# Gated recurrence and two-layer product: the first batch loaded two chunks at a time

## The chip, the cores and the metric

The kernel runs on one core of a Trainium2 chip. The metric is the device time of one launch in microseconds. A core has five engines with instruction queues of their own: TensorE (PE, with weight loads listed as PEld), VectorE (DVE), ScalarE (ACT), GpSimd (POOL) and SyncE (SP). SP here only issues DMAs, which run on sixteen DMA engines. An instruction waits in its queue for semaphores, and everything behind it on that engine waits with it.

## The reference

Batch 4, heads 8, 768 tokens, head width 48. A recurrence with a forget gate runs over the tokens, and its output goes through two matrices with `h * cos(h)` between them:

```python
f = 1.0 / (1.0 + np.exp(-f_logit))
for t in range(S):
    state = f[:, :, t, :, None] * state + np.einsum('bhd,bhe->bhde', k[:, :, t], v[:, :, t])
    y[:, :, t] = np.einsum('bhd,bhde->bhe', q[:, :, t], state)
x = y.transpose(0, 2, 1, 3).reshape(3072, 384)
h = x @ w_in            # 384 x 2048
out = (h * np.cos(h)) @ w_out   # 2048 x 384
```

## The kernel before

The recurrence is computed in 24 chunks of 128 tokens, six to a batch, numbered from 0 over all batches. For each chunk:

- `decay` loads f_logit and computes on ACT exp, then ln(1 + .), whose running sum over the tokens PE makes (`cum`); ACT then makes the decay factors `b` and their inverses `bi`. This is done for a group of chunks together, since exp and ln need another ACT table than the sine that makes the cosine. Changing the table is an instruction of its own (ACT_TABLE_LOAD).
- `attend` multiplies q by `b` and k by `bi` (`qk`, on POOL or DVE), casts v (`vb` or `vp`), turns q and k (`tr` on PE and a copy `qkt`, or a DMA transpose `tq`), multiplies them (`sc`), masks (`am`, on DVE), makes the state's update (`ps`, `st`, `sz`) and the output `y`, copies it (`yb`) and turns it to `xT` (`trx` on PE and a copy, or a DMA transpose `ty`).

`moe` takes the turned outputs by units: the first two of 128 tokens, eleven more of 256. For each of several pieces PE makes h (L651), ACT its cosine (L658), DVE the product gT (L661); then PE multiplies by w_out (`o`, L671), and ACT or DVE copies to `ot`, which is stored. The weights arrive as four quarters of each matrix in float32, in the buffers of gT, and are cast to bfloat16 (`wc`) by POOL, DVE or ACT.

Chunks below `NPAIR` = 4 have another layout: two neighbouring tokens stand in one partition, so that a contiguous piece of memory is 384 bytes instead of 192. In this layout each load is split into two DMAs of 64 partitions, four heads each, and v is spread over a zeroed tile `vp` of twice the width.

The order of work is not written by hand. `Plan` holds every operation with a cost for each engine that may do it, a priority from the table `PR`, and its buffers; `run` places them one by one in simulated time, each time choosing the engine whose operation could start first and, within `WINDOW`, the one of lowest priority. The result is a fixed order for each engine, and the program's semaphores then do the rest at run time. `GROUPS` says which chunks share their exponentials: one list entry is a group that ACT does without a cosine between, and its numbers are chunks done in one instruction. `PR["gate"]` names the cosine after which a group may begin, and from group `FREE_GROUPS` on a group waits for all its loads of f. Buffers come from `Slots` and PSUM banks from `Banks`.

```python
GROUPS = [(1, 1, 1), (1,), (2,), (2, 2), (2, 2), (2, 2), (2, 2), (2,)]
UNITS = [128, 128] + [256] * 11
TURN_QK = range(14, 23)
TURN_Y = range(12, 23)
```

`TURN_QK` and `TURN_Y` list the chunks whose q and k, or whose outputs, are turned by DMA.

Of the kernel before, what the change touches and what calls it, by code (L numbers as in the profile page):

```python
# [46 lines left out]
class Banks:  # L47
# [33 lines left out]
    def ap(self, s):  # L81
        t = self.base["tiles"][s // 2]
        return t if self.size == 2 else t[:, (s % 2) * 512:(s % 2) * 512 + 512]
# [33 lines left out]
class Plan:  # L117
# [5 lines left out]
    WINDOW = 60.0  # L123
# [4 lines left out]
    def op(self, name, eng, fn, reads=(), writes=(), prio=0.0, table=None, lat=0.0, grp=None,  # L128
           dma=None):
        o = Op()  # L130
        o.name, o.eng, o.fn, o.prio, o.table = name, eng, fn, prio, table
# [23 lines left out]
    def run(self):  # L155
        free = dict.fromkeys(("PE", "ACT", "DVE", "POOL", "SP"), 0.0)
# [10 lines left out]
        while len(order) < n:  # L167
            cand = []
            for o in ready:
# [18 lines left out]
                for e, cost in o.eng.items():  # L188
                    if e == "ACT" and lock is not None and o.grp != lock and o.table is not None:
                        continue  # L190
                    s = max(at, free[e])
                    sw = self.TABLE if e == "ACT" and o.table not in (None, table) else 0.0
                    if pick is None or s + cost + sw < pick[0]:
                        pick = (s + cost + sw, s, e, cost)
# [8 lines left out]
            if e == "ACT" and o.table is not None:  # L203
                if o.table != table:
                    s += self.TABLE
                table = o.table
                if o.grp is not None:
                    left[o.grp] -= 1
                    lock = o.grp if left[o.grp] else None
# [38 lines left out]
GROUPS = [(1, 1, 1), (1,), (2,), (2, 2), (2, 2), (2, 2), (2, 2), (2,)]  # L248
UNITS = [128, 128] + [256] * 11
NPAIR = 4  # L250
FREE_GROUPS = 1
TURN_QK = range(14, 23)
TURN_Y = range(12, 23)
PR = {
    "at": [-12.29, -6.15, -7.86, -3.54, -3.92, 15.62, -19.28, -37.09, -8.89, 2.67, 9.58, 17.38, 9.92, 20.25,
          -11.32, -1.58, 13.93, 10.35, 34.42, 26.02, 40.51, 24.64, 16.95, 12.68],
    "dec": [-8.47, -57.31, -61.04, -69.2, -28.24, -49.14, -79.64, -48.44],
    "f": [-43.16, -25.03, -22.97, -8.07, -2.31, -6.19, 24.79, 54.63, 17.72, 57.23, 51.15, 47.24, 55.46,
          53.45, 44.74, 80.64, 54.13, 111.71, 112.22, 68.31, 95.05, 72.38, 86.37, 55.7],
    "h": [3.03, 31.23, 1.72, -0.8, 2.61, 9.56, -7.84, 18.41, -24.77, 18.52, 17.84, 12.56, -12.9],  # L260
    "k": [-21.87, -16.94, -7.69, -4.47, -9.06, 6.14, 15.33, 36.65, 25.42, 15.32, 15.8, 44.24, 49.16, 72.37,
          75.37, 80.56, 68.29, 83.23, 95.28, 87.29, 95.57, 100.98, 97.99, 79.82],
    "o": [58.13, 26.04, 22.05, 54.64, 24.66, 21.51, 44.13, 47.06, 68.58, 102.72, 70.22, 82.65, 82.73],
    "tq": [1.37, -18.62, 8.94, -41.89, -22.72, -30.79, -29.34, 13.32, 0.45, 25.45, 44.49, 73.32, 0.51, 38.11,
          -19.6, -35.07, -26.72, -52.99, -63.88, -22.16, -23.59, 5.62, -39.1, -8.27],
    "ty": [-29.44, -2.23, -1.14, -18.62, -50.77, -26.99, -41.9, -38.55, -40.26, -17.32, 25.61, -2.03, 2.74,
          8.38, 49.55, 45.48, 2.91, -0.4, -39.16, -44.82, -2.61, -2.74, -26.93, -15.21],
    "v": [-26.8, -34.27, -11.26, 0.13, 3.34, 10.3, 16.09, 22.38, 43.81, 38.01, 48.41, 44.56, 41.68, 43.68,
          90.07, 49.48, 98.02, 44.19, 100.52, 65.78, 64.72, 77.22, 79.02, 126.2],
    "w_in": [-45.54, -7.28, 5.66, -12.05],  # L270
    "w_out": [6.72, 10.57, 101.81, 165.61],
    "wc": [0.78, -2, -17.61, -40.6, -45.98, 2.72, 16.43, 45.54],
    "gate": [None, None, 1, 1, 5, 20, 28, 36],
}


def build(nc, cpool, ppool, q, k, v, f_logit, moe_w_in, moe_w_out, out):
# [21 lines left out]
    if NPAIR:  # L299
        incl, strict = tl([128, 128], BF16, "incl"), tl([128, 128], BF16, "strict")  # L300
        pmask, half = tl([128, 2, 2, 64], BF16, "pmask"), tl([128, 2], BF16, "half")
    if NPAIR and nc is not None:
# [19 lines left out]
    def zpad(t):  # L322
# [3 lines left out]
    kS = slots("k", 4, [128, H, D], F32)  # L326
    qS = slots("q", 4, [128, H, D], F32)
    vS = slots("v", 4, [128, H, D], F32)
# [3 lines left out]
    qkS = slots("qk", 3, [128, 2, H, 64], zero=zpad)  # L332
    vbS = slots("vb", 4, [128, HD])
    vpS = slots("vp", 3, [128, 2, HD], zero=lambda t: nc.gpsimd.memset(t, 0.0)) if NPAIR else None
# [9 lines left out]
    w_in_bf = tl([128, KM, d_ff], BF16, "w_in_bf")  # L344
    w_out_bf = tl([128, KF, d_model], BF16, "w_out_bf")

    base = {"held": [False] * 8, "free": [0.0] * 8,
            "last": [[] for _ in range(8)], "now": [[] for _ in range(8)],
            "tiles": [ppool.tile([128, 1024], F32, name=f"ps_{i}") for i in range(4)]}
    phS = Banks(base, 2, [0, 2, 4], "ph")  # L350
    scS = Banks(base, 2, [4, 6, 2], "sc")
    p1S = Banks(base, 1, [7, 6, 5, 4, 3, 2], "p1")
# [15 lines left out]
    w_in_v = [Val(ap=w_in_bf[:, :, i * 512:(i + 1) * 512] if nc is not None else None) for i in range(NW)]  # L368
# [23 lines left out]
    def load(t, src, b, c, n, prio, nm):  # L392
        def fn(e):
            tok = src[b, :, c * C:(c + 1) * C, :]
            if n >= NPAIR:
                nc.sync.dma_start(out=t.ap, in_=tok.rearrange("h p d -> p h d"))
                return
            for r in range(2):
                (nc.scalar if e == "ACT" else nc.sync).dma_start(
                    out=t.ap[64 * r:64 * r + 64].rearrange("p (h e) d -> p h (e d)", e=2),  # L400
                    in_=tok[4 * r:4 * r + 4].rearrange("h (p e) d -> p h (e d)", e=2))
        P.op(nm + str(n), {"ACT" if nm == "q" and n == 0 else "SP": 420.0 if n >= NPAIR else 840.0}, fn,
             writes=[t], prio=prio, dma=1000.0 if n >= NPAIR else 720.0)

# [7 lines left out]

    def decay(chunks, g, prio):

        m = len(chunks)
        ft, sp, bt, bi = Val(fS), Val(spS), Val(bS), Val(biS)
        pc = Val(scS if m == 2 else p1S)
        for i, (b, c, n, ld) in enumerate(chunks):
            load(ft.part(lambda a, i=i: a[:, i]), f_logit, b, c, n, PR["f"][n], "f")
        fl = lambda a: a[:, 0:m].rearrange("p m h d -> p (m h d)")  # L420

        first = P.op("exp", {"ACT": act(384 * m, "S")}, lambda e: nc.scalar.activation(  # L422
            out=fl(ft.ap), in_=fl(ft.ap), func=AF.Exp, scale=-1.0),
# [4 lines left out]
        if g >= FREE_GROUPS:  # L428
            for o in firsts[g]:
                o.deps.update(loads)  # L430
        def ln(e):
            o, i_ = sp.ap[:, 0:m, :, 0:D], ft.ap[:, 0:m]
            if chunks[0][2] < NPAIR:
                o = sp.ap.rearrange("p m h d -> p (m h) d").rearrange(
                    "p (e h) d -> p h e d", e=2)[:, 0:4 * m, :, 0:D]
                i_ = i_.rearrange("p m h d -> p (m h) d").rearrange("p (h e) d -> p h e d", e=2)
            nc.scalar.activation(out=o, in_=i_, func=AF.Ln, bias=1.0)  # L437
        P.op("ln", {"ACT": act(384 * m, "S")}, ln, reads=[ft], writes=[sp], prio=prio, table="E", grp=g)
        cut = (lambda i: pc.ap[:, 512 * i:512 * i + 512]) if m == 2 else (lambda i: pc.ap)

        for i in range(m):
            def pe(e, i=i, pair=chunks[i][2] < NPAIR):
                o = cut(i)
                if pair:
                    rows = sp.ap.rearrange("p m h d -> p (m h) d")
                    w = rows.rearrange("p (e h) d -> p h e d", e=2)[:, 4 * i:4 * i + 4]
                    v = o[:, 0:HD].rearrange("p (h e d) -> p h e d", e=2, d=D)
                    nc.tensor.matmul(v, lhsT=incl, start=True, stop=False,  # L448
                                     rhs=w[:, :, 0:1, 0:D].broadcast_to([128, NP, 2, D]))
                    nc.tensor.matmul(v[:, :, 0, :], lhsT=strict, rhs=w[:, :, 1, 0:D], start=False, stop=False)  # L450
                    nc.tensor.matmul(v[:, :, 1, :], lhsT=incl, rhs=w[:, :, 1, 0:D], start=False, stop=False)
                    for p in range(2):
                        for e in range(2):
                            nc.tensor.matmul(o[:, HD + p:HD + NP:2], lhsT=rows[:, 8 * e + 4 * i + 2 * p:8 * e + 4 * i + 2 * p + 2, :].rearrange(
                                                 "p h d -> p (h d)"),
                                             rhs=half, start=False, stop=(p == 1 and e == 1))
# [3 lines left out]
                for p in range(NP):  # L460
                    nc.tensor.matmul(o[:, HD + p:HD + p + 1],
                                     lhsT=sp.ap[:, i, 2 * p:2 * p + 2, :].rearrange("p h d -> p (h d)"),
                                     rhs=umask[:, C - 1:C], start=False, stop=(p == NP - 1))
            P.op("cum", {"PE": 285.0 if chunks[i][2] >= NPAIR else 450.0}, pe, reads=[sp], writes=[pc], prio=prio)
# [10 lines left out]
    def attend(b, c, n, ld, bt, bi, i, prio):  # L475
        kf, qf, vf = ld
        pm = n < NPAIR
        qk, vb = Val(qkS), Val(vpS if pm else vbS)
        E = lambda e: nc.vector if e == "DVE" else nc.gpsimd
        for j, (src, dec) in enumerate(((qf, bt), (kf, bi))):  # L480
            P.op("qk", {"POOL": 1150.0, "DVE": 640.0} if n < 4 else {"POOL": 1150.0},
                 lambda e, j=j, src=src, dec=dec: E(e).tensor_mul(  # L482
                out=qk.ap[:, j, :, 0:D].rearrange("p (e h) d -> p h e d", e=2) if pm else qk.ap[:, j, :, 0:D],
                in0=src.ap.rearrange("p (h e) d -> p h e d", e=2) if pm else src.ap,
# [285 lines left out]
```

## Time and profile before

| | |
|---|---|
| median of 3 runs | 214.08 us (213.7 to 215.01) |
| the profiled execution | 213.22 us |
| its span, first to last instruction | 211.4 us |
| PE busy | 174.7 us, 83% |
| DVE busy | 137.8 us, 65% |
| ACT busy | 130.5 us, 62% |
| POOL busy | 68.7 us, 32% |
| DMA | 33.62 MB in 113237 packets, mean 159 GB/s |

Busy time is the time in which an engine executes an instruction. Matmuls overlap in the pipeline, so the busy time of PE holds latency as well as work. The clock is the share of full speed that TensorE was granted; its mean is 0.984. A line as L651 is a line of the kernel's source.

### The profile page before, as it was taken

What the parts mean: (1) busy time and instruction counts of PE and PEld (TensorE: products, weight loads), DVE (VectorE), ACT (ScalarE), POOL (GpSimd) and SP (SyncE); (2) the same over time, 40 slices, a digit from 0 to 9 for tenths busy, and PEclk for the clock granted to TensorE, in tenths of its full rate; (3) what the DMA queues carried; (4) which work ended last, traced back from release to release, by engine and by line L of the source; (5) the groups of instructions that cost most, each with busy time, mean ns of one, the idle gap of its engine ahead of it and who ended that gap; (6) DMA issues with size and microseconds to landing.
All of it is one profiled execution on the core that took longest, in us unless ns stands there. A gap on an engine that the chain in (4) does not pass through costs nothing.

```text
span 211.4 us, 4701 instructions
## 1 busy us (share of the span) xinstructions
PE 174.7 (83%) x1871; PEld 130.2 (62%) x1871; DVE 137.8 (65%) x179; ACT 130.5 (62%) x157; POOL 68.7 (32%) x108
## 2 busy tenths in 40 slices
PE   0152685678989888999989899999998999989983
PEld 0142574566757745787847657768875678857651
DVE  1825859798858963679882776845896767814400
ACT  2274279867994865295887635689687455815511
POOL 8300114820073134486007751119051711000000
PEclk9999599999999999999999999999999999999999
DMA  6969799999998988979988999845955241011113
GB/s 186 181 168 229 192 228 249 271 245 239 274 180 176 198 169 195 219 167 214 177 170 183 182 221 173 175 128 101 145 111 139 64 86 41 0 52 39 40 39 112
DMA packets 113237, 33.62 MB, mean 159 GB/s; under 512 B 106560, under 2 KB 111680, under 8 KB 113216
## 3 DMA queue, kind: packets, MB, share of 16 engines
q1 hardware_dynamic: 112672, 33.14, 71.8%
q10 hardware_dynamic: 544, 0.20, 0.5%
q8 instruction: 14, 0.23, 0.5%
q14 instruction: 7, 0.06, 0.1%
HBM read 25.17 MB, written 4.72 MB: 141 GB/s over the span
## 4 chain that ended last, share of the span: by engine, by line
PE 50%; DVE 7%; ACT 1%; issue 1%; DVEq 0%; ACTq 0%
PE ps L671 23%; PE ps L651 20%; DVE gT L661 3%; PE ps L612 1%; PE ps L550 1%; ACT ot L674 1%; DVE am L554 1%; DVE st L584 1%; PE ps L458 1%; PE ps L600 1%; PE ps L575 1%; DVE yb L525 1%; DVE qkt L525 1%; PE ps L515 1%; PE ps L630 1%
## 5 line engine op out<-in xcount | busy, mean ns | idle before, releaser
L671 PE MATMUL ps<-w_out_bf,gT 128*128 128x384 bf16 x384 | 70.1, 326 | 6.8 <-DVE st L584 2.1
L651 PE MATMUL ps<-xT,w_in_bf 128*128 128x256 bf16 (+1 forms) x624 | 69.8, 264 | 4.1 <-DVE w_in_bf L389 2.3
L661 DVE TENSOR_TENSOR gT<-ps,cosh 128x1024 bf16<-128x1024 f32 x48 | 57.9, 1219 | 14.7 <-ACT cosh L658 14.2
L658 ACT ACTIVATE cosh<-ps,halfpi 128x1024 bf16<-128x1024 f32 x48 | 52.9, 1113 | 23.1 <-PE ps L651 19.5
L651 PEld LDWEIGHTS <-w_in_bf 128*128 128x128 bf16 x624 | 55.9, 98 | 12.4 <-DVE w_in_bf L389 2.5
L671 PEld LDWEIGHTS <-gT 128*128 128x128 bf16 x384 | 35.6, 97 | 29.0 <-issue 8.5
L482 POOL TENSOR_TENSOR qk<-q,b 128x384 bf16<-128x384 f32 x21 | 21.1, 1004 | 38.1 <-ACT b L468 23.0
L590 POOL TENSOR_TENSOR sz<-st,b 64x192 bf16<-64x192 f32 x32 | 16.1, 503 | 33.1 <-DVE st L584 30.0
L554 DVE TENSOR_TENSOR am<-ps,umask 128x1024 bf16<-128x1024 f32 x20 | 24.4, 1218 | 2.9 <-ACT bi L468 1.3
L482 POOL TENSOR_TENSOR qk<-k,bi 128x384 bf16<-128x384 f32 x20 | 20.4, 1021 | 2.8 <-DMA k<-in_k_dram 2.4
L674 ACT COPY ot<-ps 128x384 f32<-128x384 f32 x16 | 7.7, 478 | 21.8 <-PE ps L671 16.7
L422 ACT ACTIVATE f<-f 128x768 f32<-128x768 f32 (+1 forms) x14 | 10.1, 747 | 9.7 <-DMA f<-in_f_logit_dram 9.6
L468 ACT ACTIVATE b<-ps 128x776 f32<-128x776 f32 (+1 forms) x14 | 10.2, 729 | 8.8 <-issue 4.6
L389 DVE CAST w_in_bf<-gT 128x1536 bf16<-128x1536 f32 x4 | 7.0, 1752 | 9.2 <-DMA gT<-in_moe_w_in_dram 9.2
L584 DVE TENSOR_TENSOR st<-ps,sz 128x384 f32<-128x384 f32 x16 | 8.8, 552 | 5.3 <-PE ps L575 2.4
L525 DVE CAST yb<-ps 128x384 bf16<-128x384 f32 x14 | 7.8, 554 | 6.6 <-PE ps L671 2.1
L389 POOL CAST vb<-v 128x384 bf16<-128x384 f32 x9 | 4.5, 503 | 20.3 <-PE ps L612 16.5
L448 PE MATMUL ps<-sp,incl 128*128 128x384 bf16 x4 | 2.0, 501 | 10.7 <-ACT sp L437 10.7
L468 ACT ACTIVATE bi<-ps 128x768 f32<-128x768 f32 (+1 forms) x14 | 10.1, 723 | 0.7 <-PE ps L511 0.7
L737 ACT ACT_TABLE_LOAD x7 | 9.0, 1283 | 2.2 <-issue 2.1
L437 ACT ACTIVATE sp<-f 128x768 bf16<-128x768 f32 (+1 forms) x14 | 10.0, 744 | 0.1
L389 DVE CAST vb<-v 128x384 bf16<-128x384 f32 x11 | 5.9, 535 | 5.3 <-PE ps L612 5.2
(68 smaller groups left out, 174.5 us busy)
## 6 DMA issues: line engine op xcount, KB each, us to landing
k<-in_k_dram SPq DMA_DIRECT2D x20, 192.0 KB, 4.2
q<-in_q_dram SPq DMA_DIRECT2D x20, 192.0 KB, 4.1
f<-in_f_logit_dram SPq DMA_DIRECT2D x20, 192.0 KB, 4.1
v<-in_v_dram SPq DMA_DIRECT2D x20, 192.0 KB, 3.7
out_dram<-ot SPq DMA_DIRECT2D x20, 192.0 KB, 2.7
gT<-in_moe_w_in_dram SPq DMA_DIRECT2D x4, 768.0 KB, 5.5
gT<-in_moe_w_out_dram SPq DMA_DIRECT2D x4, 768.0 KB, 7.3
f<-in_f_logit_dram SPq DMA_DIRECT2D x8, 96.0 KB, 3.1
```

Of the source, the lines that this page charges most:

```text
L389: (nc.scalar.copy if e == "ACT" else nc.vector.tensor_copy if e == "DVE" else nc.gpsimd.tensor_copy)(out=o, in_=i_)
L422: first = P.op("exp", {"ACT": act(384 * m, "S")}, lambda e: nc.scalar.activation(out=fl(ft.ap), in_=fl(ft.ap), func=AF.Exp, scale=-1.0), r ...
L468: nc.scalar.activation(out=out_.ap[:, 0:m, :], in_=i, func=AF.Exp, scale=s)
L482: lambda e, j=j, src=src, dec=dec: E(e).tensor_mul(out=qk.ap[:, j, :, 0:D].rearrange("p (e h) d -> p h e d", e=2) if pm else qk.ap[:, j, : ...
L525: (nc.scalar.copy if e == "ACT" else nc.vector.tensor_copy)(out=o, in_=i_)
L554: P.op("am", {"DVE": dve(1024)}, lambda e: nc.vector.tensor_mul(out=am.ap.rearrange("p r a n -> p (r a n)").rearrange("p (a n) -> p a n", ...
L584: P.op("st", {"DVE": dve(384)}, lambda e: nc.vector.tensor_add(out=st.ap, in0=pv(), in1=S_in.ap), reads=[ps, S_in], writes=[st], prio=prio)
L590: eng().tensor_mul(out=S_out.ap[s, :, r, :], in0=srcap()[s, :, r, :], in1=bt.ap[s, i, HD:, None].broadcast_to([64, NP, D]))
L651: nc.tensor.matmul(ph.ap[:, g * T:(g + 1) * T], lhsT=w_in_bf[:, m, f0:f0 + 128], rhs=x[:, m, :], start=(g % (G // 2) == 0 and m == 0), sto ...
L658: nc.scalar.activation(out=co.ap, in_=ph.ap, func=AF.Sin, bias=halfpi),
L661: P.op("g", {"DVE": dve(1024)}, lambda e, ph=ph, co=co, gv=gv: nc.vector.tensor_mul(out=gv.ap, in0=ph.ap.rearrange("p (g t) -> p g t", t=T ...
L671: nc.tensor.matmul(po.ap[:, 0:d_model], lhsT=gT.ap[:, j, i * C:(i + 1) * C], rhs=w_out_bf[:, j, :], start=(j == 0), stop=(j == KF - 1))
```

## The change

- All six chunks of batch 0 are in the paired layout, two chunks at a time (`DUALS` = 3 pairs). The two neighbouring tokens of one partition now come from a stretch of 256 tokens, so one DMA of 128 partitions and eight heads brings two chunks of a tensor. `attend2` works on such a pair; `attend` keeps the plain layout alone.
- The groups of exponentials are six, each of four chunks.
- k, q and v share a pool of 7 double buffers (`ld`) instead of 4 each, and qk has two double buffers instead of three single ones. Two more PSUM banks may be used for single-bank values.
- w_in is stored in SBUF by quarters, so that a cast writes one contiguous piece in each partition.
- q and k are turned by DMA from chunk 16 on, instead of 14; outputs from chunk 12 on, as before.
- The planner's costs, its window, its priorities and gates are others, and `PIN` fixes the engine of some operations. By this the w_in and w_out casts stand on POOL (five) and ACT (three), where DVE had seven and ACT one.

```diff
-GROUPS = [(1, 1, 1), (1,), (2,), (2, 2), (2, 2), (2, 2), (2, 2), (2,)]
+GROUPS = [(2, 2), (2, 2), (2, 2), (2, 2), (2, 2), (2, 2)]
 UNITS = [128, 128] + [256] * 11
-NPAIR = 4
+DUALS = 3
 FREE_GROUPS = 1
-TURN_QK = range(14, 23)
+TURN_QK = range(16, 23)
 TURN_Y = range(12, 23)
...
-    WINDOW = 60.0
+    WINDOW = 120.0
...
+        if PIN.get(len(self.ops)) in eng:
+            eng = {PIN[len(self.ops)]: eng[PIN[len(self.ops)]]}
...
-        free = dict.fromkeys(("PE", "ACT", "DVE", "POOL", "SP"), 0.0)
+        free = {"PE": 0.0, "ACT": 800.0, "DVE": 3500.0, "POOL": 4500.0, "SP": 750.0}
...
+    ldB = halves("ld", 7, HD, F32)
+    ldS = Banks(ldB, 1, list(range(13, -1, -1)), "ld")
+    ld2S = Banks(ldB, 2, list(range(0, 14, 2)), "ld2")
...
-    w_in_bf = tl([128, KM, d_ff], BF16, "w_in_bf")
+    w_in_bf = tl([128, d_ff // 512, KM, 512], BF16, "w_in_bf")
...
-            for r in range(2):
-                (nc.scalar if e == "ACT" else nc.sync).dma_start(
-                    out=t.ap[64 * r:64 * r + 64].rearrange("p (h e) d -> p h (e d)", e=2),
-                    in_=tok[4 * r:4 * r + 4].rearrange("h (p e) d -> p h (e d)", e=2))
...
+            else:
+                i_.dma_start(out=o.rearrange("p (h x) -> p h x", h=H),
+                             in_=src[b, :, c * C:(c + 2) * C, :].rearrange("h (p e) d -> p h (e d)", e=2))
...
+    def attend2(b, c, n, ld, bt, bi, prio):
...
+        for i in range(2):
+            for j, (src, dec) in enumerate(((qf, bt), (kf, bi))):
+                P.op("qk", {"POOL": 1150.0, "DVE": 700.0}, lambda e, j=j, i=i, src=src, dec=dec: E(e).tensor_mul(
...
+        for x in range(2):
+            piece = vb.part(lambda a, x=x: a[64 * x:64 * x + 64, x, :])
+            P.op("vb", {"POOL": 1050.0, "ACT": act(768, "S"), "DVE": 520.0}, lambda e, x=x, piece=piece:
+                 cast(e, piece.ap, vf.ap[64 * x:64 * x + 64, :]), reads=[vf], writes=[piece], prio=prio)
...
+        for i in range(2):
+            pt, qkt, sc, am = Val(p1S), Val(qktS), Val(scS), Val(amS)
...
+        P.op("ps", {"PE": mm(192, 8)}, pes, reads=[parts[1][0], parts[1][1], vb] + before, writes=[ps], prio=prio)
...
+        P.op("y", {"PE": mm(96, 24 if S[0] is not None else 20)}, pey,
+             reads=ams + [vb] + qkts + [x for x in S if x is not None], writes=[py], prio=prio)
+        for x in range(2):
+            finish(n + x, py, lambda x=x: py.ap.rearrange("p (i n) -> p i n", i=2)[:, :, 192 * x:192 * x + 192], prio)
```

A pair in `attend2` does every step for heads 0 to 3 of both chunks and then for heads 4 to 7; its output y is one PSUM value, which waits for both masks and both states, and the two chunks' outputs are copied from it one after the other.

## The prediction

> **What bounds the kernel now.** I read the busy slices first, then stretches, then the start in order of time, then the chain of work that ended last.
>
> ```profile
> PE   0152685678989888999989899999998999989983
> PEclk9999599999999999999999999999999999999999
> DMA  6969799999998988979988999845955241011113
> ```
>
> (Each digit is a fortieth of 211.4 us, in tenths.) After eight slices PE is dense, and the granted clock is full but for one slice, so what counts is when PE becomes dense. DMA is nearly full from slice 5 to 24, and falls off after.
>
> ```profile
> 0.00:45.00 45.00, 21.14 (x302) 17.81 (x303) 27.88 (x49) 24.22 (x36) 15.88 (x38) 0.92 0.92 219
> 45.00:60.00 15.00, 13.70 (x163) 10.31 (x161) 11.94 (x14) 13.11 (x15) 2.21 (x4) 1.00 0.99 235
> 60.00:115.00 55.00, 50.04 (x557) 37.29 (x555) 39.95 (x53) 37.87 (x46) 24.59 (x33) 1.00 0.91 188
> 115.00:208.20 93.20, 89.82 (x856) 64.83 (x854) 58.05 (x65) 54.78 (x62) 25.97 (x35) 1.00 0.50 102
> ```
>
> (Columns: stretch, length, busy us of PE, weight load, DVE, ACT, POOL, clock, DMA share, GB/s.) PE is idle for 23.9 of the first 45 us and for 9.6 of the next 163.
>
> Busy time in the start is inflated by latency, so I price PE work by the dense pieces of the chain:
>
> ```profile
> 118.99 2.62 PE ps L651 x24
> 121.61 0.17 PE ps L575 x4
> 121.78 0.65 PE ps L671 x4
> 122.43 0.33 PE ps L550 x8
> ```
>
> That is 109 ns for a matmul of h (half for the two 128-token units), 162 ns for one of o, 41 to 42 ns for the small ones; likewise 0.45 us for eight transposes of qk, 0.26 for a cumulative sum, 0.17 to 0.20 for each part of y. Over all instructions this is 162.0 us of work, and PE ends at 208.2: **46.2 us are lost**. By 45 us only 84 matmuls of h and the attention of three and a half chunks are done, 15.2 us of work: 29.8 us lost there, 2.0 to 60 us, 8.4 to 115, 6.0 to the end.
>
> Why the start is slow:
>
> ```profile
> 0.73 0.45 SPq L383 DMA_DIRECT2D gT<-in_moe_w_in_dram  x1
> 1.24 1.42 SPq L399 DMA_DIRECT2D f<-in_f_logit_dram  x2
> 7.56 0.52 ACT L422 ACTIVATE f<-f 128x384 f32<-128x384 f32 x1 [4.14 <-DMA f<-in_f_logit_dram]
> 9.25 2.59 SPq L399 DMA_DIRECT2D k<-in_k_dram  x4
> 15.66 0.56 DVE L482 TENSOR_TENSOR qk<-q,b 128x384 bf16<-128x384 f32 x1 [1.63 <-DMA q<-in_q_dram]
> 27.09 0.84 PE L651 MATMUL ps<-xT,w_in_bf 128*128 128x128 bf16 x12
> 43.67 2.87 PE L651 MATMUL ps<-xT,w_in_bf 128*128 128x256 bf16 x24 [0.91 <-DVE xT L525]
> ```
>
> (Start, duration.) The first w_in quarter goes ahead of the first f, so exp begins at 7.56. Each 96 KB half load takes SP 0.65 us to issue, 150 KB per us. Between 10 and 15 us the DMA share is only 0.68: SP's issuing is the limit. The first h is at 27.1, unit 2 (chunks 2 and 3) at 43.7.
>
> **The change part by part.** Durations are from the rows of before; the order of the changed program is known.
>
> *Loads.* A load of two chunks over 128 partitions is one issue for 384 KB. Four replace sixteen half loads for each of the first two pairs; chunks 4 and 5 need four instead of eight. With two fewer qk transposes SP and ACT issue some 140 DMAs instead of 168. Packets of 384 bytes took 23 ns uncrowded and 36 to 40 crowded in the DMA records, so 1024 on 16 engines take 1.4 to 1.9 us (1.7 taken).
>
> A rule that speaks against this edit's worth: the Trainium skill (DMA: Bandwidth & Descriptors, Rules for kernel authors) says that transfers to the two partition halves share the same engines[...]. By the rule alone the edit is worth issue time only. But the row shows that issue time is the limit: at 0.68 share, one third of the capacity is unused. So I count the issue time and no more: the bytes still cost 1.7 us per load.
>
> *Pair 0.* Order: f, v, k, q, then w_in 0. First packets at 2.0 (before: 1.9). f lands near 5.1 (1.3 us after its last packet, as before), exp at 5.2 instead of 7.56. exp and ln of 768 columns, 0.84 each: 6.9. Fourteen matmuls of sums, 1.8: 8.8. b and bi, 0.82 each: 10.6. q lands 9.1 to 10.8. DVE multiplies q and k to 12.4 with POOL's share beside it. Sixteen transposes (1.0 per eight when cold): 13.5. ps x8 1.5: 15.0. Two state updates, then two masks of 1.22: 18.3. y x20, cold: 20.2. Two copies, six transposes, xT: **first h at 22.2** instead of 27.1, with both chunks.
>
> *Pair 1.* h x36, ps and 16 transposes: 26.7. ACT has a table load (1.28), a cosine (1.1) and two qkt (1.0 each): 28.3. Masks behind st and the gate on DVE: 30.7. y x24: 32.3. yb, six transposes, xT: 34.3. With 1.5 us for waits that I don't see, **unit 2 starts near 36** instead of 43.7, and its h (48 x 109 ns) ends near 41.5. Work done by then: 10.5 of h, 8.8 of two pairs, 19.3 us. Lost: 22.2.
>
> *w_in by quarters, casts moved.* Four w_in casts (1.75) and three of w_out (1.13) leave DVE; five go to POOL and two more to ACT (1.47 for its one in before). POOL has no such row: its 384-column cast takes 0.50, so 1.7 (0.1 fixed) to 2.0 by proportion; I take 2.0. Quarter 0 lands near 12 and is cast by 14, quarter 3 by 31 on ACT: both before use. Hidden, at nothing; without cover 2 us each.
>
> A rule speaks against it: the Trainium skill (SBUF — State Buffer, Terms) says that DVE and GpSimd share a port pair, held for a whole instruction, and the loser fully blocks. Five casts of 2.0 could by this block DVE for 10 us. The trace:
>
> ```profile
> 32.08 1.00 POOL L482 TENSOR_TENSOR qk<-q,b 128x384 bf16<-128x384 f32 x1 [0.68 <-DMA q<-in_q_dram]
> 32.24 1.25 DVE L482 TENSOR_TENSOR qk<-k,bi 128x384 bf16<-128x384 f32 x1
> 38.99 1.22 DVE L554 TENSOR_TENSOR am<-ps,pmask 128x1024 bf16<-128x1024 f32 x1
> ```
>
> The multiply that reads SBUF alone took 1.25 instead of 0.55. The mask, which reads PSUM, took its usual 1.22 while POOL was busy. So only collisions with SBUF-only work cost, 0.7 us each; I have put one in each pair. By the rule's worst case I would add 8 us and have no gain.
>
> *Chunk pair 2 and groups.* Exponentials now come in six groups instead of eight: two table loads fewer, 2.6 us of ACT, off the chain. Group 1 (chunks 4 to 7) starts exp after the eighth cosine and a table load, near 45. Its last f has ten pair loads, six weight quarters (2.1) and four chunk loads (1.0) ahead, so lands near 37: in time. From there to chunk 5's xT takes as long as pair 0 did from exp (17 us at the start, less here with PE warm: 14.5), so 59.5. PE fills this with 64 matmuls of o (10.4), pair 2 (4.5) and chunks 6 and 7 (2.1): 17 of 18 us. **Lost by 59.5: 23.2**, where before had lost 31.8.
>
> *More PE work.* Eight transposes for each of chunks 14 and 15 (0.9) since they no longer go by DMA; the paired forms for chunks 4 and 5 add sums 0.4, ps 0.5, y 0.35. Total 162.0 + 2.1 = 164.1. The outputs are turned by DMA from chunk 12 on in both programs: nothing changes there. POOL's and SP's later orders change, but the chain after 83 us is half PE and hardly ever a load.
>
> *The sum.* 164.1 of work + 23.2 + what is lost later. Before lost 14.4 after 60 us; the last small group is gone, so I take 14.0. PE ends at 201.3. From PE's end to the span's end 3.2 (copy 0.48, store 2.7), as before: 204.5. Outside the span the profiled execution has 213.22 - 211.4 = 1.8: 206.3. The runs' median lies 0.9 above the profiled execution, so **207.2** on the runs' scale, 3.2% less than 214.08.
>
> **Rivals.**
>
> A. *The lead is given back to the loads.* For: DMA share 0.91 in 60 to 115 us, with POOL waiting 11.7 us for q. Against: PE's waits after 60 us name DVE and ACT, and the longest is 1 us. If loads set the pace, only saved DMA time counts: two qk transposes of 1.7 (1024 packets of 26 ns) and 1 to 2 on chunks 4 and 5. Then 214.1 less 4 for these, plus PE's 2.1: **212.2**.
>
> B. *The tail of losses shrinks too.* DVE is about 9 us lighter, and six groups give fewer stops. If half of 14 goes: **200.2**.
>
> C. *Slower: groups of four starve PE.* A group holds ACT for two table loads (1.28) and eight activations (0.82): 9.1 us without a cosine. There are five such groups instead of four. Cover is 10.4 us of o for four chunks, if it is kept for that moment. If each of the five leaves PE idle 3 us more than I have counted, 15 us come on top of 207.2: **222.2**. It decides from 1.4 us per group ((214.1 - 207.2) / 5). For: 53 to 62 us in before is such a stop, with 0.86 idle. Against: before has four of them, and lost 14.4 in all.
>
> That the change does nothing is excluded by the order: the first h comes with both chunks' data.
>
> **How the numbers follow.** Likeliest 0.58 (own range 203 to 211: loads 1.4 or 1.9 us, POOL casts, waits of up to 4 us); A 0.15; B 0.15; C 0.12. Within 1% is about what this kernel's measurement can tell from nothing (212 to 216). Faster: 0.57 + 0.15 + 0.05 of A = 0.77; same 0.01 + 0.10 = 0.11; slower 0.12. The range that leaves out half of C and of B, and the ends of the likeliest: 199.5 to 215.
>
> **What would show it.** Right: exp near 5.2; first h near 22; unit 2's h near 36; PE's busy digits at 8 or 9 two slices earlier; DMA share near 1 from 2 to 45 us; SBUF-only work on DVE above 1.2 beside POOL. Wrong: unit 2 after 40; PE waiting for the casts or for q; or PE's idle time after 60 us above 13 us, with cosines late in each group.

## The result, and the profile after

The changed kernel takes **202.54 us** (median of 4 runs, 202.38 to 203.74) where the kernel before took 214.29 on the same chip: a ratio of 0.946, with an interval of 0.9415 to 0.951. The profiled execution took 202.38 us, with a span of 200.6. The forecast was 207.2, so the direction was right and the gain was larger than forecast: 11.8 us instead of 6.9. Medians here count every run, while the ratios leave out slow runs, those over 1.5% above the fastest run of the same kernel.

The busy slices of the kernel after (each digit a fortieth of 200.6 us, in tenths):

```profile
PE   0387979998986999998997989999899999999992
PEclk9999999999999999999999999999999999999999
DMA  6999899999799798999979588993538102120122
```

Before, PE first reached 8 in the sixth slice, fell back to 5 and held 8 or more from the tenth on; now it reaches 8 in the third slice and then stays at 6 or more up to the last one. The slice with half the clock is gone. The DMA engines fell back to 6 in the third slice of before; now they stand at 8 or 9 from the second to the tenth.

The same stretches as before the change (columns: stretch, length, busy us of PE, weight load, DVE, ACT, POOL, clock, DMA share, GB/s):

```profile
0.00:45.00 45.00, 32.51 (x404) 26.43 (x405) 30.45 (x52) 31.55 (x34) 19.96 (x35) 1.00 1.01 262
45.00:60.00 15.00, 13.61 (x182) 10.68 (x181) 12.75 (x18) 8.32 (x12) 7.26 (x10) 1.00 1.00 205
60.00:115.00 55.00, 49.91 (x564) 37.41 (x563) 38.46 (x48) 44.21 (x51) 23.46 (x32) 1.00 0.90 189
115.00:197.40 82.40, 78.86 (x771) 57.78 (x767) 52.94 (x59) 47.14 (x55) 23.12 (x31) 1.00 0.44 92
```

The first 45 us hold 404 matmuls instead of 302, and DMA moves 262 GB/s there instead of 219. The stretch from 60 to 115 us is almost what it was: PE 49.9 of 55 us busy (before 50.0), DMA share 0.90 (before 0.91). The gain was made at the start and kept.

The prediction's prices for PE work give the same account for both programs:

| us | before | after | difference |
|---|---|---|---|
| PE work by the prices | 162.0 | 164.0 | +2.0 |
| lost by 60 us | 31.8 | 19.9 | -11.9 |
| lost from 60 us to PE's end | 14.4 | 13.2 | -1.2 |
| from PE's end to the span's end | 3.2 | 3.5 | +0.3 |
| span | 211.4 | 200.6 | -10.8 |

The start of the kernel after, in order of time (start, duration, engine, line, operation, count, and in brackets the idle time before it and what ended it):

```profile
0.74 0.46 SPq L415 DMA_DIRECT2D f<-in_f_logit_dram  x1
3.08 1.24 SPq L415 DMA_DIRECT2D ld<-in_q_dram  x1
4.64 0.84 ACT L441 ACTIVATE f<-f 128x768 f32<-128x768 f32 x1 [2.62 <-DMA f<-in_f_logit_dram]
9.15 0.56 DVE L549 TENSOR_TENSOR qk<-ld,b 128x384 bf16<-128x384 f32 x1 [2.24 <-DMA ld<-in_q_dram]
9.63 1.81 DVE L549 TENSOR_TENSOR qk<-ld,bi 128x384 bf16<-128x384 f32 x2
11.21 1.56 POOL L405 CAST w_in_bf<-gT 128x1536 bf16<-128x1536 f32 x1 [0.65 <-DMA gT<-in_moe_w_in_dram]
20.71 2.23 PE L721 MATMUL ps<-xT,w_in_bf 128*128 128x128 bf16 x36
```

One issue of half a microsecond now brings f for two chunks. The first exponential starts at 4.64 us (before 7.56, and for one chunk only), and the first h at 20.71 (before 27.09).

### The profile page after: what moved, and what is told of

It reads as the page before. It is cut to its first block, busy times and chain, and to the rows that moved or that the text cites. A ratio compares the mean times of both kernels' runs of the same rounds, so it can differ in the third digit from the quotient of the medians.

```text
span 200.6 us, 4718 instructions
## 1 busy us (share of the span) xinstructions
PE 174.9 (87%) x1911; PEld 132.3 (66%) x1911; DVE 134.6 (67%) x174; ACT 131.4 (66%) x149; POOL 73.8 (37%) x107
## 4 chain that ended last, share of the span: by engine, by line
PE 68%; ACT 9%; DVE 9%; DMA 6%; issue 3%; POOL 1%; SPq 1%; ACTq 0%; POOLq 0%
PE ps L721 29%; PE ps L741 25%; DMA ld<-in_q_dram 3%; DMA ld<-in_v_dram 3%; ACT cosh L728 2%; PE ps L669 2%; ACT qkt L429 2%; DVE am L588 2%; PE ps L569 2%; DVE qkt L429 1%; PE ps L627 1%; PE ps L699 1%; PE ps L476 1%; ACT L810 1%; ACT f L441 1%
## 5 line engine op out<-in xcount | busy, mean ns | idle before, releaser
L721 PE MATMUL ps<-xT,w_in_bf 128*128 128x256 bf16 (+1 forms) x624 | 66.7, 264 | 0.4 <-ACT ot L744 0.4
L638 POOL TENSOR_TENSOR qk<-ld,b 128x384 bf16<-128x384 f32 x18 | 18.2, 1015 | 17.3 <-DMA ld<-in_q_dram 12.7
L744 ACT COPY ot<-ps 128x384 f32<-128x384 f32 x14 | 6.5, 483 | 19.9 <-PE ps L741 17.0
L638 POOL TENSOR_TENSOR qk<-ld,bi 128x384 bf16<-128x384 f32 x18 | 18.3, 1021 | 0.0
L441 ACT ACTIVATE f<-f 128x768 f32<-128x768 f32 x12 | 10.1, 838 | 5.7 <-DMA f<-in_f_logit_dram 5.6
L429 DVE COPY qkt<-ps 128x1024 bf16<-128x1024 bf16 x11 | 7.4, 685 | 7.9 <-PE ps L656 5.8
L485 ACT ACTIVATE b<-ps 128x776 f32<-128x776 f32 x12 | 9.8, 816 | 3.7 <-PE ps L479 1.5
L429 ACT CAST yb<-ps 128x384 bf16<-128x384 f32 x11 | 5.1, 481 | 9.4 <-PE ps L699 3.5
L744 DVE COPY ot<-ps 128x384 f32<-128x384 f32 x10 | 5.5, 555 | 7.4 <-PE ps L741 6.6
L456 ACT ACTIVATE sp<-f 128x768 bf16<-128x768 f32 x12 | 10.1, 844 | 0.3
L485 ACT ACTIVATE bi<-ps 128x768 f32<-128x768 f32 x12 | 9.7, 808 | 0.0
```

The costliest lines, as they stand in the source:

```text
L429: (nc.scalar.copy if e == "ACT" else nc.vector.tensor_copy)(out=o, in_=i_)
L485: nc.scalar.activation(out=out_.ap[:, 0:m, :], in_=i, func=AF.Exp, scale=s)
L638: P.op("qk", {"POOL": 1150.0}, lambda e, j=j, src=src, dec=dec: E(e).tensor_mul(out=qkv()[:, j, :, 0:D], in0=HB(src.ap), in1=HB(dec.ap[:, ...
L721: nc.tensor.matmul(ph.ap[:, g * T:(g + 1) * T], lhsT=w_in_bf[:, f0 // 512, m, f0 % 512:f0 % 512 + 128], rhs=x[:, m, :], start=(g % (G // 2 ...
L744: P.op("ot", {"ACT": act(384), "DVE": dve(384)}, lambda e, po=po, ot=ot: (nc.scalar.copy if e == "ACT" else nc.vector.tensor_copy)(out=ot. ...
```

## The experiments

Two accounts stood against each other after the result. In the first, the start is earlier because f no longer stands behind a weight quarter and because SP issues less. In the second, the shape of the transfers counts by itself: 128 partitions at once instead of two halves. The rivals of the prediction that place the gain or the loss after 60 us were already out by the table above. Each ratio below is to the kernel before on the same chip.

### Two transfers of 64 partitions for each load of a pair

```diff
-i_.dma_start(out=o.rearrange("p (h x) -> p h x", h=H),
-             in_=src[...].rearrange("h (p e) d -> p h (e d)", e=2))
+for r in range(2):
+    s = slice(64 * r, 64 * r + 64)
+    i_.dma_start(out=o.rearrange("p (h x) -> p h x", h=H)[s],
+                 in_=src[...].rearrange("h (p e) d -> p h (e d)", e=2)[s])
```

> The changed kernel with each load of two chunks (batch 0) issued as two DMAs of 64 partitions; bytes, packets of 384 bytes and the order stay. Theory (issuing on SP was the limit of the start): two issues of about 0.6 us for 384 KB are 300 KB per us, just what the DMA engines moved at 5 to 20 us, so at most 1.5 us: 202.5 to 204. Rival (half-partition transfers are slower in themselves, whatever their number): as much as in the next run, +4 or more.

Measured: 209.12 us (208.84 to 210.76), ratio 0.977, 0.971 to 0.984. That is some 3% more than the kernel after, far above the 202.5 to 204 of the first account and in the range of its rival. The first account alone doesn't explain it: each of these transfers holds 197 KB and took SP 0.65 us, which allows 300 GB/s. What was moved is shown below.

### Four transfers, the shape of before

The edit is the same with a second loop, over heads 0 to 3 and 4 to 7: 64 partitions and four heads each, as the kernel before loads.

> The changed kernel with each load of two chunks issued as four DMAs of 64 partitions and four heads, the shape and count that the kernel before had. Theory (issuing is the limit): sixteen issues of 0.65 us stand before the end of the first q load, which lands near 13 us instead of 9.1; pair 1's q some 5 us later; first h near 24.5 instead of 20.7; total +4 to +6, 206.5 to 208.5, DMA rate near 150 KB per us from 5 to 20 us. Rival (the gain comes from the order and the groups, not from how loads are issued): under +1, 203.5 at most.

Measured: 217.81 us (215.45 to 218.4), ratio 1.014, 1.007 to 1.021. This is far above both forecasts. With transfers of the shape of before, the changed program is slower than the kernel before: all else in the change (order, groups, pools, casts) keeps none of the gain. That holds for this order, which was planned for whole loads; an order planned for small ones was not run, nor was the kernel before with whole loads.

The stretch from 5 to 10 us, first in the kernel after, then with two halves, then with four pieces, each with the part from 5 to 7 us (columns as above):

```profile
5.00:10.00 5.00, 1.63 (x14) 1.16 (x13) 2.73 (x7) 3.67 (x5) 0.80 (x1) 1.00 1.20 302
5.00:7.00 2.00, 0.59 (x3) 0.40 (x3) 1.87 (x5) 1.94 (x3) 0.00 (x0) 1.00 1.28 261
8.50:9.50 1.00, 0.00 (x0) 0.00 (x0) 0.35 (x1) 1.00 (x2) 0.30 (x1) 1.00 1.03 375
```

```profile
5.00:10.00 5.00, 1.63 (x14) 1.16 (x13) 1.87 (x5) 3.56 (x5) 0.00 (x0) 1.00 1.32 203
5.00:7.00 2.00, 0.00 (x0) 0.00 (x0) 1.80 (x5) 1.45 (x2) 0.00 (x0) 1.00 1.32 202
20.00:25.00 5.00, 3.90 (x39) 3.52 (x37) 2.40 (x5) 3.10 (x4) 2.88 (x4) 0.50 1.25 238
```

```profile
5.00:10.00 5.00, 1.63 (x14) 1.17 (x13) 1.87 (x5) 2.99 (x4) 0.00 (x0) 1.00 0.67 150
5.00:7.00 2.00, 0.00 (x0) 0.00 (x0) 1.32 (x4) 0.88 (x2) 0.00 (x0) 1.00 0.68 153
```

The last two columns have to be read together. (The share is the sum of the packets' times over 16 engines, and passes 1 where packets overlap.) Packets have to be compared with packets of the same size. By the DMA records, the stretch from 5 to 10 us of the kernel after ends with the first w_in quarter, in packets of 2048 bytes, which move 375 GB/s from 8.5 to 9.5 us. From 5 to 7 us every packet has 384 bytes in all these programs. There the engines are as full with two halves as in the kernel after, 1.32 against 1.28, but they move 202 GB/s instead of 261, and a packet takes 40 ns instead of 30 (means): the transfer itself is slower. With four pieces the share is only 0.68, so the engines stand idle: 98 KB for each 0.65 us that SP spends on an issue is 150 GB/s, about what was moved.

The program with halves also has a stretch at a clock of 0.50 (20 to 25 us), which the kernel after does not have. The 36 matmuls of its first h, at 22.80 us, took 3.86 us instead of 2.23. So 1.6 us of the loss went with the lower clock. What lowered it was not tested.

### The number of transfers apart from their shape

The two runs above change both the number and the partitions. These two split by heads alone, so that each transfer keeps all 128 partitions, two or four to a load. They ran with the unchanged kernel after once more on their chip as a control.

```diff
+for g in range(2):          # range(4) with 2 heads each in the other
+    u = slice(4 * g, 4 * g + 4)
+    i_.dma_start(out=o.rearrange("p (h x) -> p h x", h=H)[:, u],
+                 in_=src[...].rearrange("h (p e) d -> p h (e d)", e=2)[:, u])
```

The control:

> The changed kernel once more, on the chip of the other runs here: 202.5, ratio to before 0.94 to 0.952.

Two transfers:

> The changed kernel with each load of two chunks issued as two DMAs of all 128 partitions and four heads each. Theory (a transfer over half the partitions moves fewer bytes per us, 203 instead of 302 GB/s at 5 to 10 us in the run with partition halves, while two issues of 0.6 us for 384 KB would still do): the DMA rate stays near 290 GB/s, and the time is 202.5 to 204.5. Rival (the number of DMAs costs, in issue time or because only so many may be under way, whatever their shape): 208 to 210, like the run with partition halves.

Four transfers:

> The changed kernel with each load of two chunks issued as four DMAs of all 128 partitions and two heads each. Both theories say that SP's issuing (four times 0.6 us for 384 KB, 160 GB/s) now sets the pace of the start. If shape costs on top of it, this is faster than the four quarters of 64 partitions (217.8): 211 to 215. If number alone counts: 217 to 218.

Measured: the control 203.75 us (201.89 to 204.39), ratio 0.948, 0.942 to 0.954. Two transfers 203.57 (203.34 to 204.93), ratio 0.946, 0.940 to 0.952. Four transfers 208.1 (207.46 to 210.13), ratio 0.967, 0.960 to 0.975. Their stretches, two transfers and then four:

```profile
5.00:10.00 5.00, 1.63 (x14) 1.16 (x13) 2.23 (x6) 3.32 (x5) 0.80 (x1) 1.00 1.10 293
5.00:7.00 2.00, 0.94 (x8) 0.65 (x8) 1.34 (x5) 1.03 (x3) 0.00 (x0) 1.00 1.14 282
```

```profile
5.00:10.00 5.00, 1.63 (x14) 1.17 (x13) 1.87 (x5) 3.87 (x5) 0.00 (x0) 1.00 0.88 193
5.00:7.00 2.00, 0.39 (x2) 0.22 (x2) 1.49 (x5) 1.72 (x3) 0.00 (x0) 1.00 0.88 193
```

Two transfers came out as the account by shape forecast; four were faster than either account said.

Together with the runs before they make a table of two causes (ratio to the kernel before; GB/s from 5 to 7 us; start of VectorE's multiply that waits for q, and of the first h, in us):

| transfers for a pair's load | 128 partitions each | 64 partitions each |
|---|---|---|
| one | 0.946; 261 GB/s; q 9.15, h 20.71 | |
| one, the control | 0.948; 261 GB/s; q 9.04, h 19.50 | |
| two | 0.946; 282 GB/s; q 9.65, h 19.70 | 0.977; 202 GB/s; q 11.48, h 22.80 |
| four | 0.967; 193 GB/s; q 11.39, h 22.93 | 1.014; 153 GB/s; q 14.90, h 25.76 |

Two transfers cost nothing in time if they keep all partitions, and 3% if they are halves. Four cost 2% by their number: 98 KB for each issue of 0.50 us is 197 GB/s, and 193 were moved. With 64 partitions as well, an issue takes 0.65 us. Two halves and four whole transfers bring q and the first h at nearly the same time; the halves lose more behind it, with unit 2's h at 36.4 us against 34.8, around the stretch at half the clock. Both causes are shown, and taking both away costs more than the whole gain. Part of that comes behind the start: with four pieces of 64 partitions, PE waits 5.2 us once for a cast of w_out on POOL.

What makes a transfer of 64 partitions slow was not taken apart. The Trainium skill (SBUF — State Buffer, Door 1: The DMA port swizzle) says that one half of the partitions reaches only half of the ports through which DMA writes SBUF, and gives 196 GB/s for 64 partitions against 328 for 128, measured with 1 MiB. The 202 GB/s here, with transfers to both halves under way, agree with the first figure; the 261 of whole loads, in packets of 384 bytes, lie below the second.

### The order of f and the first weight quarter

In the kernel after, the first w_in quarter is issued before everything else again, as in the kernel before:

```diff
+w0 = next(o for o in order if o.name == "w01")
+order.remove(w0)
+order.insert(0, w0)
```

> The changed kernel with the first w_in quarter issued ahead of f, as before had it. Theory (the start is one chain from f's landing): f lands 2.1 us later (768 KB), exp near 6.7, and all of it follows: +1.5 to +2.5, 204 to 205. Rival (transfers later in the start or POOL's cast set the pace, so the quarter has to come anyway): 0 to +0.5, since the quarter lands earlier by as much.

Measured: 207.56 us (204.97 to 209.02), ratio 0.960, 0.953 to 0.968: some 3 us more than the kernel after, with an interval that touches the control's. The first exponential started at 7.18 us instead of 4.64. Its profiled execution is the slowest of its four runs, so its inner times aren't compared here. The order is worth between nothing and 5 us, most likely about 3, once loads are whole.

The reverse, in the kernel before: the quarter behind chunk 1's q, and its cast before that of the next quarter.

```diff
+w0 = next(o for o in order if o.name == "w00")
+order.remove(w0)
+order.insert(order.index(next(o for o in order if o.name == "q1")) + 1, w0)
+wc = sorted((o for o in order if o.name == "wc"), key=lambda o: o.seq)
+order.remove(wc[0])
+order.insert(order.index(wc[3]), wc[0])
```

> The kernel before with its first w_in quarter issued behind the q load of chunk 1 instead of ahead of f; its cast on DVE stands just before the cast of the second quarter, behind the products q, k of chunks 0 and 1. Theory (issuing is the limit there): exp comes near 5.5 instead of 7.56, but the q and k loads still come at one per 1.3 us on SP, only 0.5 us earlier, and the two quarters now stand together before the first state update: -0.5 to +1.5, 213.5 to 215.5. Rival (the order of f and w_in is what the start gained by): -2, 212.

Measured: 215.02 us (213.78 to 216.98), ratio 1.001, 0.998 to 1.005. The first exponential started at 5.66 us instead of 7.56, and the first h at 27.00 instead of 27.09: nothing of the 1.9 us arrived. The order of time in this program shows where it went (VectorE's rows):

```profile
14.47 0.55 DVE L482 TENSOR_TENSOR qk<-k,bi 128x384 bf16<-128x384 f32 x1
16.71 1.75 DVE L389 CAST w_in_bf<-gT 128x1536 bf16<-128x1536 f32 x1 [1.68 <-DMA gT<-in_moe_w_in_dram]
19.02 1.75 DVE L389 CAST w_in_bf<-gT 128x1536 bf16<-128x1536 f32 x1 [0.56 <-DMA gT<-in_moe_w_in_dram]
20.69 0.34 DVE L590 TENSOR_TENSOR sz<-ps,b 64x192 bf16<-64x192 f32 x1
```

The multiply comes 1.7 us earlier than before, but then VectorE stands at two weight casts whose quarters have not landed, and sz, which is queued behind them, starts at 20.69 us, as before (20.78). So this run can't say whether the small loads set the pace, or only the casts at the head of VectorE's queue.

### The casts out of the way in the kernel before

Two more runs on the kernel before were made to tell these apart. Quarter 1 is loaded in place of quarter 3 and the other way round; these casts, and chunk 2's cast of v, stand behind the masks and products of the first chunks on VectorE. The second run also has f first.

```diff
+am, qk, wc = dve("am"), dve("qk"), dve("wc")     # VectorE's, in its order
+vp = next(o for o in dve("vb") if order.index(o) > order.index(dve("sz")[0]))
+a, b = (order.index(named(x)) for x in ("w03", "w01"))
+order[a], order[b] = order[b], order[a]
+behind(vp, am[1])
+behind(wc[2], qk[5])
+behind(wc[1], qk[6])
+behind(named("w00"), named("q1"))    # these two in the second run alone
+behind(wc[0], am[1])
```

The casts alone:

> In the kernel before, VectorE had the cast of w_in's quarter 3, and the cast of chunk 2's v, ahead of the first decay of the state (sz); it stood idle 2.4 us for that quarter, and sz came at 20.8 us although its inputs were there near 15.4. Here quarter 1 is loaded in place of quarter 3 and the other way round, and these casts stand behind the masks and products of the first chunks; f still comes behind the first quarter. If the half loads set the pace of the start (my theory), the first h moves from 27.1 to about 23.5 us, but chunk 2's q is issued at 21.6 us as before, so unit 2's h stays within 2 us of 43.7 and the time within 1.5 us of before (ratio 0.993 to 1.003). If the casts at the head of VectorE's queue were a cause of their own (rival), unit 2's h comes 3 us or more earlier and the ratio is 0.985 or less.

The casts, and f first:

> As the kernel with the casts later, and f ahead of the first w_in quarter as well, in the kernel before with its half loads. By the earlier run f ahead alone gave nothing since VectorE stood at the casts. Theory (half loads set the pace): first h near 21.7 us, unit 2's h within 3 us of 43.7, ratio 0.985 to 1.000. Rival (order and casts could have given much of the gain without another shape of loads): unit 2's h at 39 us or earlier, ratio 0.975 or less.

Measured: 239.76 us (238.94 to 240.13), ratio 1.115, 1.110 to 1.120; and 239.01 us (238.62 to 239.12), ratio 1.112, 1.108 to 1.116. Quarter 3's cast now stands behind the first products that use the quarter, so these are made with other weights, and VectorE stood 25 us at that cast for a transfer of w_out. So these times answer neither expectation. What comes before that cast, up to 32 us, can be read. In the run with the casts alone sz starts at 16.96 us and the second mask ends at 21.6, three us earlier than before; yet the first h is at 26.29, not near 23.5 (with f first as well: 25.86). The next load of f, from SP's issue to the first h, and SP's wait in that issue:

```profile
17.17 3.69 SPq L399 DMA_DIRECT2D f<-in_f_logit_dram  x2
23.30 0.52 ACT L422 ACTIVATE f<-f 128x384 f32<-128x384 f32 x1 [3.78 <-DMA f<-in_f_logit_dram]
23.73 0.46 ACT L525 CAST yb<-ps 128x384 bf16<-128x384 f32 x1
26.29 1.44 PE L651 MATMUL ps<-xT,w_in_bf 128*128 128x128 bf16 x12
...
SPq L399 <- ACT qkt L525: 2.4, 1, 2.4
```

ACT's queue holds chunk 3's exponential ahead of yb, and its f, whose two halves SP starts to issue at 17.17 us, lands at 23.3. So with the casts away most of the lead stops at a load, and 0.8 us of it reaches the first h. But the shape of that load is not what made it late. Its first half stood 3.0 us in SP's queue, where most halves take 0.6, and by the profile 2.4 of them were a wait for ACT's copy qkt (2.2 in the kernel before). Chunk 2's q, which SP issues behind this f, came no earlier than before either (its multiply at 26.30, before 25.07). These two runs therefore show an order in which one queue holds another, casts on VectorE first and then this f on SP and ACT; they do not show that the small loads alone held the start of the kernel before. What such an order would do to the whole time was not measured.

### Casts on VectorE, the layout of w_in, and the turned chunks

With the loads whole again: the five weight casts of POOL put on DVE, at the same places of the order:

```diff
-o.fn(o.eng)
+o.fn("DVE" if o.name == "wc" and o.eng == "POOL" else o.eng)
```

> The changed kernel with the five weight casts of POOL issued on DVE, at the same place in the order. Theory (on POOL they are hidden, on DVE they stand in the chain): five casts of 0.95 to 1.1, two of them before unit 2, +1 to +3: 203.5 to 205.5. Rival (on POOL they hold DVE back through the shared port by as much): 0, or faster by up to 1.

Measured: 205.13 us (203.52 to 206.99), ratio 0.950, 0.942 to 0.958, against 0.948 for the control. The intervals overlap for most of their length, so this doesn't tell a gain from none.

w_in stored as one block of 2048 columns, so that a cast writes three strided pieces in each partition:

```diff
-w_in_bf = tl([128, d_ff // 512, KM, 512], BF16, "w_in_bf")
+w_in_bf = tl([128, KM, d_ff], BF16, "w_in_bf")
...
-lhsT=w_in_bf[:, f0 // 512, m, f0 % 512:f0 % 512 + 128]
+lhsT=w_in_bf[:, m, f0:f0 + 128]
```

> The changed kernel with w_in stored in SBUF as in the kernel before (a quarter is three pieces of 512 columns, not one of 1536). Theory (the layout of w_in counts for its casts alone, and these are hidden on POOL and ACT): no difference from the changed kernel within 0.6%, 202 to 204. Rival (the strided cast takes POOL or ACT much longer, as DVE's 1.75 against 1.13 us suggests, and holds up the first h): +1 to +2, casts above 2 us.

Measured: 204.27 us (204.25 to 205.03), ratio 0.951, 0.946 to 0.955: not told apart from the control. The casts' own durations answer the question directly (ns: least, median, most; first and last start in us; size). The kernel after, this one, the one with casts on DVE (by quarters), and the kernel before (DVE, one block):

```profile
L405 POOL CAST w_in_bf<-gT x2: 1465/1513/1561, 11.2 to 18.6; 128x1536 bf16<-128x1536 f32 x2
```

```profile
L405 POOL CAST w_in_bf<-gT x2: 1464/1464/1464, 11.8 to 18.9; 128x1536 bf16<-128x1536 f32 x2
```

```profile
L405 DVE CAST w_in_bf<-gT x2: 947/948/950, 11.3 to 19.6; 128x1536 bf16<-128x1536 f32 x2
```

```profile
L389 DVE CAST w_in_bf<-gT x4: 1752/1752/1753, 5.6 to 37.3; 128x1536 bf16<-128x1536 f32 x4
```

On POOL and ACT (1477 in both) the layout makes no difference. On DVE it does: 1.75 us into strided pieces, 0.95 into a contiguous one. The changed kernel has no w_in cast on DVE, so it doesn't use this.

q and k of chunks 14 and 15 turned by DMA again, with no transposes on PE:

```diff
-lambda e: cp(...)        # qkt of chunks 14 and 15, a copy on DVE or ACT
+lambda e: nc.sync.dma_start_transpose(out=qkt.ap, in_=qk.ap)
```

> The changed kernel with q and k of chunks 14 and 15 turned by DMA, issued on SP where the copy from PSUM stood in the order; PE loses sixteen transposes (0.9 us of dense work) and ACT or DVE two copies (0.7 to 1.0 each). Theory (PE is the limit after 60 us, so its work counts): -0.5 to -0.9, which is at the edge of what can be told. Rival (the DMA lands some 3 us after its issue, where transposes and copy took 1.5, and SP's queue waits for qk): +0.5 to +2.

Measured: 203.21 us (202.82 to 205.0), ratio 0.947, 0.940 to 0.954: no difference. The work by the prices fell from 164.0 to 163.1 us and in the profiled execution PE's end did not come earlier (198.2 against 197.1): the saved 0.9 us of PE turned into losses.

## Why the prediction was right in direction and short in size

**What was right.** The start bounds the kernel; the saving there stays. Of 10.8 us less span, 11.9 were lost less by 60 us. The step on more PE work (164.1 in the sum) measured 164.0. Losses after 60 us, taken as 14.0, measured 13.2. The tail, taken as 3.2, measured 3.5, and the time outside the span was 1.8 as taken. The DMA share of the first 45 us was 1.01, near the 1 that was forecast (0.92 before).

**What failed: a term put at nothing.** The prediction let the shape of a transfer cost nothing, "I count the issue time and no more". The row of before (DMA share 0.68) did show a limit by issues, but it was read as the only one. Earlier in the kernel before, halves had filled the engines and moved little, at the share and the rate of the run with two halves (1.32 and 202), which was there to be read:

```profile
5.00:7.00 2.00, 0.00 (x0) 0.00 (x0) 1.36 (x1) 0.00 (x0) 0.85 (x2) 1.00 1.34 206
```

The prediction's inference from the Trainium skill (DMA: Bandwidth & Descriptors, Rules for kernel authors), that whole loads are worth issue time only, does not hold in these runs (261 GB/s against 202). The row's advice, one transfer of 128 partitions, does.

**What this did to the number is less.** The price of a load, 1.7 us, was worked out from packets of half loads, 23 to 40 ns. (64 of them on each engine, one after another, would be 1.5 to 2.6 us; the range of 1.4 to 1.9 needs packets that overlap, which the prediction doesn't say.) Whole loads landed 1.5 us apart: f's exponential starts at 4.64 us and, three loads later, the multiply that waits for q at 9.15, inside the 9.1 to 10.8 that were given. That a price taken from half loads came so near is in part luck. The miss of 4.7 us is made of many small terms:

| step | predicted | measured |
|---|---|---|
| first exponential | 5.2 us | 4.64 |
| first h | 22.2 | 20.71 |
| unit 2's h | near 36 | 31.9 |
| lost by 60 us | 23.2 | 19.9 |
| lost later | 14.0 | 13.2 |
| PE's end | 201.3 | 197.1 |

The first h came 1.5 us early: 0.6 are f's landing, 0.4 the steps from the exponential to `bi`, the rest smaller. From the first h to unit 2 it took 11.2 us instead of 13.8. The largest mis-sized term stands here: the 1.5 us "for waits that I don't see" were not needed. The first h, products and transposes of this pair took 3.8 us instead of 4.5, and the masks and y 0.4 less each. Of these 4.1 us, 3.3 were left by 60 us. With 0.8 lost less later and 0.1 less work they are the 4.2 us at PE's end. The other 0.5 us came from the step to the runs' scale: 0.9 was added, but the median lies only 0.2 above the profiled execution, and the tail was 0.3 longer.

Such small leads at the start are not a measure of the whole time. The control's first h came at 19.50 us and its unit 2 at 30.66, both 1.2 us before the other execution's, and it took 0.4 us longer (202.82 against 202.38).

The step "cold" came true: the sixteen transposes at 10.61 us took 1.89 us, those of the second pair, at 23.44, 1.06. The granted clock doesn't show this; it stands at 1.00 in both places.

Two lines show the h of the first two chunks and of unit 2 (three matmuls for each 128 columns; the last row holds 12 of a unit of 128 tokens and 48 of unit 2):

```profile
20.71 2.23 PE L721 MATMUL ps<-xT,w_in_bf 128*128 128x128 bf16 x36
...
30.99 6.38 PE L721 MATMUL ps<-xT,w_in_bf 128*128 128x128 bf16 x60
```

Unit 2 starts inside the last row, 0.9 us after its start, 4 us earlier than forecast.

**The casts and the port.** POOL's casts, taken at 2.0 us, took 1.47 to 1.56 and stayed hidden in the profiled execution; in the control PE waited once for one of w_out, 1.7 us. The multiply on DVE that reads SBUF took up to 1.37 us beside POOL's work and 0.56 without it, as in the row of before. Its price was right, and so was its small weight. What the prediction did not see is that in the kernel before a cast on VectorE, waiting for its quarter, held sz 3.8 us (20.78 against 16.96 with it away); it counted the moved casts as hidden work and nothing else. What this was worth in time isn't known.

**The rivals.** A (given back to the loads): refuted, since 60 to 115 us is unchanged with the lead kept, though POOL still waits for q, off PE's path. B (the losses later halve): refuted, 14.4 became 13.2. C (groups of four starve PE): refuted; PE's longest waits are these, and both of the long ones lie in the first 11 us:

```profile
PE ps L467 <- ACT sp L456: 6.4, 1, 6.4
PE ps L569 <- POOL qk L549: 2.6, 1, 2.6
PE ps L741 <- DVE ot L744: 1.3, 2, 0.6
```

Rival C needed more than 1.4 us at each of five groups; no wait after the first pair reaches that in this execution. The control's one wait of 1.7 us is for a cast of w_out.

**What stays open.** Why the clock fell with halves, and how its 1.6 us and the slower transfer act together. How much the casts on POOL are worth in time. In the kernel before, the casts at the head of VectorE's queue held the start up to 20.7 us and the issue of one f on SP behind them; how much of the start was then the pace of the small loads, and what another order would have given to the whole time with the loads as they were, is not known.

## What to carry to other kernels

At a start that waits for data, look at the shape of the early loads as well as at their order: here all 128 partitions in a transfer and 197 KB or more in each lost nothing to issuing, while 98 KB did. Read the DMA share together with the GB/s, and compare packets of one size: here a share of 0.68 at 153 GB/s was an issue limit, and one of 1.32 at 202 GB/s a transfer of poor shape, and the two have different cures. A stretch that mixes packets of 384 and 2048 bytes (261 and 375 GB/s here) can make a difference of shape look larger than it is. Price the start by the chain of the first landing (f, exponential, sums, q, the first product): of the 11.9 us won by 60 us, 10.8 were left in the span, with 2.0 more work done.

## What was not expected of the hardware

From 5 to 7 us, where every packet had 384 bytes, transfers to 64 partitions kept the DMA engines at a share of 1.32 and moved 202 GB/s; transfers to 128 partitions moved 261 at 1.28 and, split in two by heads, 282 at 1.14. Issuing on SP cost 0.50 us for a transfer of 128 partitions with two or four heads and 0.65 for one of 64 partitions with four or eight heads, in each pair without regard to its bytes. A cast of 128x1536 from float32 to bfloat16 took 1.46 to 1.56 us on POOL, 1.48 on ACT and 0.95 on DVE, with contiguous and with strided destination alike on POOL and ACT; DVE took 1.75 with the strided one. PE's transposes took nearly twice as long at 10 us as at 23 (1.89 and 1.06 us for sixteen) at a granted clock of 1.00 both times.
